# Raw attention pairs as four TensorE blocks, and TensorE in written order from the start: a sparse-attention and feed-forward kernel on one Trainium2 core

## The chip, the cores and the metric

The kernel runs on one core of a Trainium2 chip. The core has a matrix engine (TensorE, PE in the rows), a vector engine (VectorE, DVE), a scalar engine (ScalarE, ACT), a general engine (GpSimd, POOL) and a queue that starts transfers (SyncE, SP). Each engine works through its own list of instructions in the order in which they stand there, and waits on semaphores for the others. Matrix products go to PSUM, which has eight banks of 512 fp32 columns by 128 partitions; all other operands lie in SBUF. TensorE's clock is granted at one of two levels, 1.2 or 2.4 GHz.

The metric is the device time of one execution in microseconds (us), lower is better. The kernel before takes 1020.98 us, the median of three runs (1018.97 to 1024.09).

## The reference

Eight batches with eight heads each, head size 64. Each head has 512 local and 32 global tokens. A local token sees the 32 global ones and the local ones at a distance of up to 32; a global token sees all. The result of all heads is one row of 512 numbers per token, which goes through a feed-forward network with 2048 hidden units and a slope `alpha` for negative values.

```python
k_all = concatenate([k_g, k_l]); v_all = concatenate([v_g, v_l])
out_g = softmax(q_g @ k_all.T / 8) @ v_all
s_ll = where(abs(pos_q - pos_k) <= 32, q_l @ k_l.T / 8, -1e9)
out_l = softmax(concatenate([q_l @ k_g.T / 8, s_ll])) @ v_all
x = heads side by side, 4352 rows of 512
h = x @ w_in                              # 512 x 2048
g = maximum(h, 0) + alpha * minimum(h, 0)
return g @ w_out                          # 2048 x 512
```

## The kernel before

**The feed-forward part** is most of the work. The tokens form nine groups: the 512 local tokens of each batch, and at the end all 256 global ones. A group has 16 steps, one per 128 hidden units. Step `t` issues `f1(t)` (12 matmuls of 128 rows by 512 columns into a bank `h`: x and `w_in` are each split into a high and a low part, and three of the four products are added), then VectorE, ScalarE and GpSimd make `gh` and `gl` of it, and two steps later `f2(t)` (12 matmuls) adds into the four banks `o0` to `o3`. There are two `h` banks, two `s` banks for all of attention, and four `o` banks: eight in all.

**Weights.** There are 32 pieces of weights (f, j), each loaded as 64-bit words, decoded by two ScalarE, three VectorE and one GpSimd instruction (`decode_words`, L113 to L120), and split by one ScalarE and one GpSimd instruction (`split_weights`, L126, L127). `weights_step` decodes 11 pieces before step 0 and the other 21 in the first 14 steps.

**Attention** is done in pairs `P` of heads, 32 pairs, four to a batch. The main loop runs over units `u`; unit `u` holds step `t = u - 19`, so 19 units (the prelude) go ahead of step 0. Pair `P` begins in unit `4P`. The pairs 0 to 7 are "raw": they work in plain fp32 and transpose the probabilities on TensorE; the pairs from 8 on use another route, which the change leaves as it is. The pairs 0 to 3 are finished in the prelude, 4 to 7 in the first 17 steps.

A raw pair does the following. (1) Scores: for each of two heads and four chunks of 128 queries, two matmuls of 64 x 64 by 160 columns (`s_ps`), then a VectorE instruction that scales, masks and finds the minimum (L243), a ScalarE exponential (L247), a sum, a reciprocal (L209) and a ScalarE scaling (L214) into `p_sb`. Before, one unit does two chunks of one head in one bank, so a pair takes four score blocks in four units. (2) Eight TensorE transposes of `p_sb` (`pt`, L313), copied to `pt_sb` by ScalarE (L302), and VectorE transposes of the rest (L318). (3) The scores of the global tokens (`g_ps`) and their softmax in `sg_sb` (L270 to L280), two TensorE transposes of it (L286) and two copies. (4) The products with v (`pv_raw`, 24 matmuls into `o_ps`, in two halves in two units), and copies to `x_raw` and `x_glb`. `p_sb`, `pt_sb` and `sg_sb` exist once: pair P+1 can write each only when pair P has been read.

**What sets the order.** The program is traced unit by unit: `attn_pre`, `f1`, `attn_mid`, `f2` part 0, `attn_post`, `f2` part 1, `weights_step`. A scheduler with a timeline of its own then fixes each engine's list; what is inside `boost(u)` is preferred. From unit 36 on (`pinned`, `PIN`), the matmuls of the helper at L92 keep the order in which they are written; before that, and for the transposes, the scheduler may move them. In the prelude `keep_warm` issues four matmuls of zeros by 512 columns in each of 18 units, into the `h` banks.

```python
EV = dict(pt0=(2, "mid"), pt1=(4, "pre"), ptg=(4, "pre"), pv0=(5, "mid"), pv1=(6, "mid"))
BT = dict(s="s", g="o3", o="s", w="h")
```

These two lines give the unit of each raw event relative to `4P`, and the bank of each kind (in the prelude the transposes take `o0` to `o2`; from pair 4 on all take `s`).

## Time and profile before

| | |
|---|---|
| median of the runs | 1020.98 us |
| profiled execution | 1023.57 us |
| span of its trace | 1021.8 us |
| mean granted clock of TensorE | 0.979 of 2.4 GHz |
| TensorE busy with matmuls | 990.6 us, 97% |
| VectorE, ScalarE, GpSimd busy | 61%, 52%, 40% |

The span runs from the first to the last instruction of the trace; the execution's own time is 1.8 us longer. A matmul's busy time overlaps that of its neighbours, so steps are best read from start to start: in the steady part eight matmuls of 512 columns start 1.87 us apart in all, 0.234 us each. In a row of the timeline the first number is the start, the second the time to the end of the last instruction of the row, then engine, line and operation, `out<-in`, for a matmul rows x columns of the loaded block, the shape, and the count. An fp32 matmul of a raw pair appears as two passes, so a score block of four matmuls is a row with x8. A bracket gives the idle time ahead of the row and what ended it.

### The profile page before, as it was taken

The page shows a single profiled execution, that of the slowest core. Times are in us where ns is not written, and L with a number is a line of the kernel's source. Part 1 is how long each engine was busy: PE and PEld are TensorE (multiplying, and loading weights), DVE is VectorE, ACT ScalarE, POOL GpSimd, SP SyncE. Part 2 cuts the span into 40 slices and gives each one's busy share as a digit, 9 for nine tenths or more (in the row PEclk, how much of TensorE's full clock was granted, in tenths as well). Part 3 has the DMA queues.
Part 4 walks back from the last instruction along what each step waited for, and adds up shares of the span by engine and source line. Part 5 has one row for each costly group of instructions (what it writes and reads, how often), then busy time and mean ns, then how long its engine had stood idle before and what let it go on. Part 6 is the DMA issues. An engine that isn't in the chain of part 4 may idle for free.

```text
span 1021.8 us, 16979 instructions
## 1 busy us (share of the span) xinstructions
PE 990.6 (97%) x5592; PEld 793.0 (78%) x5592; DVE 625.8 (61%) x1999; ACT 532.9 (52%) x1491; POOL 413.5 (40%) x333
## 2 busy tenths in 40 slices
PE   7998998988999999999999999999999999999998
PEld 4565766766888888888888888888888888888798
DVE  7946868766666766676666666766667665322322
ACT  6767665675555655555556555555556543201121
POOL 6712666664344343334344344334434422222222
PEclk9897999989999999999999999999999999999999
DMA  9725233226454554555445544555455532100010
GB/s 348 263 65 209 94 113 115 70 65 192 140 152 140 169 152 146 149 155 175 140 146 158 181 143 143 151 160 156 130 152 177 154 109 86 42 1 1 1 42 22
DMA packets 95273, 133.00 MB, mean 130 GB/s; under 512 B 10192, under 2 KB 53712, under 8 KB 95184
## 3 DMA queue, kind: packets, MB, share of 16 engines
q1 hardware_dynamic: 95184, 131.91, 41.5%
q8 instruction: 44, 0.72, 0.3%
q14 instruction: 45, 0.37, 0.1%
HBM read 100.93 MB, written 30.93 MB: 129 GB/s over the span
## 4 chain that ended last, share of the span: by engine, by line
PE 85%; DVE 8%; ACT 4%; issue 2%; POOL 1%; DMA 0%; SPq 0%; DVEq 0%; POOLq 0%; ACTq 0%
PE o L93 35%; PE h_ps L93 35%; PE o_ps L93 6%; PE s_ps L93 5%; PE g_ps L93 3%; DVE wt L115 1%; DVE wt L118 1%; ACT p_sb L247 1%; PE warm L93 1%; DVE pt_sb L318 1%; DVE wt L117 1%; ACT wt L113 1%; DVE g L405 1%; DVE p_sb L243 0%; DVE g L406 0%
## 5 line engine op out<-in xcount | busy, mean ns | idle before, releaser
L93 PE MATMUL h_ps<-xh,wt 128*128 128x512 f32 (+1 forms) x1152 | 352.3, 388 | 1.4 <-DVE g L406 1.4
L409 POOL TENSOR_TENSOR gl<-g,gh 128x512 fp32r<-128x512 f32 (+1 forms) x144 | 178.4, 1239 | 422.7 <-ACT gh L408 377.2
L93 PE MATMUL o<-gh,wt 128*128 128x512 f32 (+1 forms) x1152 | 284.5, 389 | 5.1 <-ACT ost L302 3.6
L93 PEld LDWEIGHTS o<-gh,wt 128*128 128x128 f32 x1152 | 207.7, 190 | 52.5 <-ACT ost L302 4.6
L93 PEld LDWEIGHTS h_ps<-xh,wt 128*128 128x128 f32 x1152 | 207.3, 191 | 41.9 <-DVE g L406 1.7
L93 PE MATMUL h_ps<-xl,wt 128*128 128x512 f32 (+1 forms) x576 | 222.4, 387 | 1.0 <-DVE xl L388 0.9
L408 ACT CAST gh<-g 128x512 fp32r<-128x512 f32 (+1 forms) x144 | 85.4, 593 | 251.9 <-DVE g L406 243.7
L405 DVE TENSOR_SCALAR g<-h_ps,alpha_sb 128x512 f32<-128x512 f32 (+1 forms) x144 | 103.2, 717 | 142.3 <-PE h_ps L93 139.2
L93 PE MATMUL o<-gl,wt 128*128 128x512 f32 (+1 forms) x576 | 151.6, 384 | 0.0
L247 ACT ACTIVATE p_sb<-p_sb,mn 128x224 f32<-128x224 f32 (+2 forms) x256 | 115.1, 451 | 53.6 <-DVE mn L243 53.5
L214 ACT ACTIVATE p_sb<-p_sb,rz 128x192 f32<-128x192 f32 (+1 forms) x252 | 101.5, 452 | 70.6 <-DVE rz L209 64.9
L93 PEld LDWEIGHTS h_ps<-xl,wt 128*128 128x128 f32 x576 | 109.1, 190 | 26.1 <-DVE xl L388 1.8
L93 PEld LDWEIGHTS o<-gl,wt 128*128 128x128 f32 x576 | 104.9, 188 | 24.0 <-issue 0.6
L297 DVE STREAM_TRANSPOSE pt_sb<-sg_sb 32x64 f32<-32x64 f32 x384 | 90.5, 236 | 26.8 <-ACT sg_sb L280 21.5
L193 POOL TENSOR_TENSOR hi<-rawq,hi 64x512 fp32r<-64x512 f32 x48 | 62.4, 1300 | 90.5 <-DMA vt<-in_vt_dram 53.3
L406 DVE SCALAR_TENSOR_TENSOR g<-h_ps,g 128x512 f32<-128x512 f32 (+1 forms) x144 | 94.0, 653 | 3.0
L243 DVE CUSTOM_DVE_ANT_0 p_sb<-s_ps,mask 128x192 f32<-128x192 f32 x192 | 65.2, 369 | 28.8 <-PE s_ps L93 25.3
L196 POOL TENSOR_TENSOR kl<-rawk,hi 128x640 fp32r<-128x640 f32 x48 | 75.4, 1571 | 3.7
L93 PE MATMUL o_ps<-pt_sb,vt 128*64 128x160 f32 (+4 forms) x832 | 69.5, 289 | 2.7 <-ACT pt_sb L302 1.1
L209 DVE RECIPROCAL rz<-rz 128x2 f32<-128x2 f32 x128 | 20.8, 164 | 76.7 <-ACT rz L208 75.6
L93 PEld LDWEIGHTS o_ps<-pt_sb,vt 128*64 128x64 f32 (+2 forms) x832 | 49.4, 135 | 22.2 <-issue 14.8
L120 POOL TENSOR_TENSOR wt<-wt,wr 128x512 int32<-128x512 int32 x32 | 42.8, 1339 | 45.5 <-DVE wt L118 31.0
(85 smaller groups left out, 1055.0 us busy)
## 6 DMA issues: line engine op xcount, KB each, us to landing
scratch<-p_sb SPq DMA_DIRECT2D x192, 112.0 KB, 2.4
wraw<-in_w_dram SPq DMA_DIRECT2D x32, 512.0 KB, 7.1
vt<-in_vt_dram SPq DMA_DIRECT2D x32, 512.0 KB, 4.7
rawk<-in_qk_dram SPq DMA_DIRECT2D x96, 160.0 KB, 3.0
rawq<-in_qk_dram SPq DMA_DIRECT2D x96, 128.0 KB, 2.7
pt_sb<-scratch SPq DMA_DIRECT2D x48, 256.0 KB, 2.7
gn<-in_gn_dram SPq DMA_DIRECT2D x32, 304.0 KB, 4.9
pt_sb<-scratch SPq DMA_DIRECT2D x48, 192.0 KB, 2.9
```

What stands on the lines that cost most here:

```text
L93: ins = nc.tensor.matmul(*a, **k)
L120: nc.gpsimd.tensor_tensor(ti, ti, r, op=ALU.add)
L193: nc.gpsimd.tensor_tensor(q, raw[64:128], q.bitcast(F32), op=ALU.subtract)
L196: nc.gpsimd.tensor_tensor(kl[P, h], raw, t.bitcast(F32), op=ALU.subtract)
L214: nc.scalar.activation(r, r, AF.Copy, scale=rz[:parts, e : e + 1])
L243: nc.vector.tensor_tensor_reduce(out=pr, in0=s[:, 256 * e : 256 * e + nn], in1=masks[e], scale=-0.125, scalar=3.0e38, op0=ALU.add, op1=ALU ...
L247: nc.scalar.activation(pr, pr, AF.Exp, bias=mn[:, e : e + 1], scale=-1.0, accum_out=z[:, e : e + 1])
L297: nc.vector.transpose(dst, src)
L405: nc.vector.tensor_scalar(g[:, 0:n], h[:, 0:n], 0.0, alpha_sb[:, f : f + 1], op0=ALU.min, op1=ALU.mult)
L406: nc.vector.scalar_tensor_tensor(g[:, 0:n], h[:, 0:n], 0.0, g[:, 0:n], op0=ALU.max, op1=ALU.add)
L408: nc.scalar.copy(gh[:, 0:n], g[:, 0:n])
L409: nc.gpsimd.tensor_tensor(gl[:, 0:n], g[:, 0:n], gh[:, 0:n].bitcast(F32), op=ALU.subtract)
```

## The change

A raw pair becomes four blocks, one per unit, each with two whole banks, all in `attn_mid`. Unit `4P`: the scores of chunks 0, 1 and 2 of both heads, head 0 in one bank and head 1 in the other. Unit `4P+1`: chunk 3 of both heads, and in the second bank the two transposes of the previous pair's `sg_sb`. Unit `4P+2`: all products with v of the previous pair and this pair's global scores (the banks that the later pairs already use in that way). Unit `4P+3`: all eight transposes, one bank per head. In the prelude the blocks take `o0,o1`, `s,s`, `o2,o3`, `s,s` in turn; later all take the two `s` banks. All matmuls and transposes of the whole program keep their written order. The zeros become five matmuls in each of 19 units (95 in place of 72), behind the unit's block. A pair's softmax gets one sum and one reciprocal for six chunks and one for two; GpSimd scales three chunks of pair 0 in place of four.

```diff
-NWARM = 18
-WARM = (2, 2)
+NWARM = 19
+WARM = 5
-PIN = 36
     def matmul(*a, **k):
-        ins = nc.tensor.matmul(*a, **k)
-        if pinned[0]:
-            tc.keep_in_program_order(ins)
-        return ins
+        tc.keep_in_program_order(nc.tensor.matmul(*a, **k))
+
+    def transpose(*a):
+        tc.keep_in_program_order(nc.tensor.transpose(*a))
...
+    def pair_banks(u, names):
+        tags = {0: ("o0", "o1"), 2: ("o2", "o3")}.get(u % 4, "ss") if u < NPRE else "ss"
+        return [bank(tag, name) for tag, name in zip(tags, names)]
...
+    def scores_raw(P, chunks, banks):
+        for y, i in enumerate(chunks):
+            for h in range(2):
+                t = hi[P][64 * h : 64 * h + 64]
+                for f in range(2):
+                    q0, k0 = 128 * i + 64 * f, NQ + 160 * i + 64 * f
+                    matmul(banks[h][64 * f : 64 * f + 64, 160 * y : 160 * y + 160], t[:, q0 : q0 + 64], t[:, k0 : k0 + 160], start=True, stop=True)
...
+    def values_and_globals(P):
+        first, last = held.pop(P)
+        if live(P - 1):
+            (pv_raw if P - 1 < NRAW else pv_all)(P - 1, first, last)
+        if live(P):
+            global_scores(P)
+        if live(P - 1):
+            pv_out(P - 1, first, last)
...
+    def raw_block(u):
+        P, s = divmod(u, 4)
+        raw, glb = live(P) and P < NRAW, 0 <= P - 1 < NRAW
+        if s == 0 and raw:
+            banks = pair_banks(u, ("s_ps", "s_ps"))
+            scores_raw(P, (0, 1, 2), banks)
+            softmax_raw(P, (0, 1, 2), banks)
+        if s == 1 and (raw or glb):
+            banks = pair_banks(u, ("s_ps", "s_ps"))
+            if raw:
+                scores_raw(P, (3,), banks)
+            if glb:
+                transpose_glb(banks[1])
+            if raw:
+                softmax_raw(P, (3,), banks)
+            if glb:
+                copy_glb(banks[1])
+                global_transposes(P - 1)
+        if s == 3 and raw:
+            banks = pair_banks(u, ("pt", "pt"))
+            for h in range(2):
+                transpose_pe(h, banks[h])
+            for h in range(2):
+                copy_pe(h, banks[h])
...
     def attn_mid(u):
         P, s = divmod(u, 4)
-        glob(P, s, "mid")
-        while tails:
-            tails.pop()()
-        raw_events(u, "mid")
+        if s == 2 and (live(P) or live(P - 1)):
+            values_and_globals(P)
+        raw_block(u)
...
-        if u < NWARM:
-            keep_warm(WARM[0])
...
         if u < NWARM:
-            keep_warm(WARM[1])
+            keep_warm(WARM)
```

The first place is TensorE's list in the prelude, about pair 2 (`pt` are the transposes of `p_sb`, `s_ps<-ident` those of `sg_sb`). Before:

```order
L93 MATMUL s_ps<-qk_raw 64x160 x4
L93 MATMUL warm<-idle 128x512 x2
L93 MATMUL o_ps<-pt_sb,vt 64x96
L93 MATMUL warm<-idle 128x512 x2
L93 MATMUL s_ps<-qk_raw 64x160 x4
L93 MATMUL warm<-idle 128x512 x2
L313 MATMUL pt_509<-ident,p_sb 128x128 x2
L93 MATMUL warm<-idle 128x512 x10
L93 MATMUL g_ps<-gn 64x256 x2
L93 MATMUL g_ps<-gn 64x32
L93 MATMUL warm<-idle 128x512 x2
L313 MATMUL pt_509<-ident,p_sb 128x128 x2
```

The same place now:

```order
L84 MATMUL warm<-idle 128x512 x5
L87 MATMUL pt<-ident,p_sb 128x128 x8
L84 MATMUL warm<-idle 128x512 x5
L84 MATMUL s_ps<-qk_raw 64x160 x12
L84 MATMUL warm<-idle 128x512 x5
L84 MATMUL s_ps<-qk_raw 64x160 x4
L87 MATMUL s_ps<-ident,sg_sb 128x128 x2
L84 MATMUL warm<-idle 128x512 x5
L84 MATMUL o_ps<-pt_sb,vt 64x96 x2
L84 MATMUL o_ps<-pt_sb,vx 64x64 x2
L84 MATMUL o_ps<-pt_sb,vt 64x2x64 x2
L84 MATMUL o_ps<-pt_sb,vt 64x96 x2
```

The score blocks, which stood singly between warm-ups, are now one of twelve matmuls and one of four, the eight transposes stand together, every block has five warm-ups behind it, and the products with v follow the two transposes of `sg_sb`.

The second place is VectorE's list in the prelude at the end of the eleven weight pieces (`wt`, `wraw`; the last is the last of the L118 or L112 rows). Before:

```order
L357 TENSOR_REDUCE xgt<-o_ps 128x32
L270 TENSOR_REDUCE gm<-g_ps 128x1
L243 ISA p_sb,mn<-s_ps,rmask 128x160
L243 ISA mn 128x1
L243 ISA p_sb,mn<-s_ps,rmask 128x160
L243 ISA mn 128x1
L118 SCALAR_TENSOR_TENSOR wt<-wraw,wt 128x512
L358 TENSOR_TENSOR x_glb<-x_glb,xgt 128x32
L209 RECIPROCAL rz<-rz 128x2
L271 TENSOR_SCALAR gm<-gm 128x1
L243 ISA p_sb,mn<-s_ps,rmask 128x160
L243 ISA mn 128x1
```

Now:

```order
L109 TENSOR_SCALAR wt<-wt 128x512
L111 TENSOR_SCALAR wt<-wt 128x512
L112 SCALAR_TENSOR_TENSOR wt<-wraw,wt 128x512
L211 RECIPROCAL rz<-rz 128x6
L211 RECIPROCAL rz<-rz 128x2
L315 STREAM_TRANSPOSE pt_sb<-p_sb 32x4x32 x6
L366 TENSOR_REDUCE x_glb<-o_ps 128x32
L367 TENSOR_TENSOR x_glb<-x_glb,g_ps 128x32
L267 TENSOR_REDUCE gm<-g_ps 128x1
L268 TENSOR_SCALAR gm<-gm 128x1
L269 COPY gm<-gm 64x1
L270 TENSOR_TENSOR gm<-gm 64x1
```

Behind the last weight piece there stood scores of pair 2 (the ISA rows of `mn`) and the rest of pair 1's global softmax; now there stand the reciprocals and transposes of pair 1 first, and its whole global softmax behind the outputs of pair 0.

The third place is TensorE's list among the feed-forward steps (`h_ps` is f1, `o0` to `o3` are f2). Before, at scores of pair 6 and transposes of pair 5:

```order
L93 MATMUL h_ps_1602<-xl_1028,wt_1311 128x512
L93 MATMUL h_ps_1602<-xh_1031,wt_1311 128x512 x2
L93 MATMUL s_ps_1500<-qk_raw_1209 64x160 x4
L313 MATMUL pt1_1511<-ident_114,p_sb_71 128x128 x2
L93 MATMUL h_ps_1602<-xl_1032,wt_1311 128x512
L93 MATMUL h_ps_1602<-xh_1035,wt_1311 128x512 x2
L93 MATMUL h_ps_1602<-xl_1036,wt_1311 128x512
L93 MATMUL h_ps_1602<-xh_1079,wt_1311 128x512 x2
L93 MATMUL h_ps_1602<-xl_1080,wt_1311 128x512
L93 MATMUL o0_1285<-gh_1463,wt_1013 128x512
L313 MATMUL pt1_1511<-ident_114,p_sb_71 128x128 x2
L93 MATMUL o0_1285<-gh_1463,wt_1013 128x512
```

Now, at the second block of pair 5, between f1 and f2 of one unit:

```order
L84 MATMUL h_ps_1229<-xh_1057,wt_664 128x512 x2
L84 MATMUL h_ps_1229<-xl_1058,wt_664 128x512
L84 MATMUL s_ps_1249<-qk_raw_938 64x160 x2
L84 MATMUL s_ps_1250<-qk_raw_938 64x160 x2
L87 MATMUL s_ps_1250<-ident_114,sg_sb_73 128x128 x2
L84 MATMUL o0_1268<-gh_1110,wt_381 128x512 x2
L84 MATMUL o1_1269<-gh_1110,wt_381 128x512 x2
L84 MATMUL o2_1270<-gh_1110,wt_381 128x512 x2
L84 MATMUL o3_1271<-gh_1110,wt_381 128x512 x2
L84 MATMUL o0_1268<-gl_1111,wt_381 128x512
L84 MATMUL o1_1269<-gl_1111,wt_381 128x512
L84 MATMUL o2_1270<-gl_1111,wt_381 128x512
```

Attention stood at several places inside `f1` and `f2`; now one block stands between them, and the chunk's four matmuls alternate between two banks. From the first score block of pair 9 on, TensorE's list is the same in both programs.

## Rows read from the trace of the kernel before

**Rows 1.** Of the page: the busy time of each engine.

```profile
PE 990.6 (97%) x5592; PEld 793.0 (78%) x5592; DVE 625.8 (61%) x1999; ACT 532.9 (52%) x1491; POOL 413.5 (40%) x333
```

**Rows 2.** The view of stretches (start:end, length, busy time and instructions of PE, PEld, DVE, ACT and POOL, granted clock as a share of 2.4 GHz, DMA share, GB/s): the decoding of the first weights, the pairs 1 to 3 of the prelude from one end of the products with v to the next, the steps 2 to 15, and the steady part.

```profile
20.00:40.00 20.00, 18.20 (x112) 11.43 (x111) 19.26 (x48) 17.15 (x49) 14.29 (x13) 1.00 0.77 291
...
34.40:62.90 28.50, 26.95 (x153) 16.66 (x152) 18.55 (x61) 18.99 (x61) 14.72 (x11) 0.82 0.48 173
62.90:74.90 12.00, 11.86 (x106) 7.83 (x104) 6.91 (x35) 10.43 (x39) 1.29 (x1) 1.00 0.32 98
74.90:86.60 11.70, 10.05 (x101) 6.32 (x99) 6.94 (x38) 9.32 (x35) 1.27 (x1) 1.00 0.46 149
96.40:226.00 129.60, 119.84 (x691) 89.92 (x689) 96.22 (x232) 84.17 (x214) 87.23 (x66) 0.93 0.27 91
262.00:900.00 638.00, 638.00 (x3513) 523.87 (x3512) 404.04 (x1373) 340.65 (x958) 244.40 (x180) 1.00 0.48 143
```

**Rows 3.** TensorE's timeline: the start of f1(2), the price of f1 and f2 (eight matmuls of `f2`, and the next matmul), and the first score block of pair 9.

```profile
96.43 1.22 PE L93 MATMUL h_ps<-xh,wt 128*128 128x512 f32 x2
...
197.03 2.03 PE L93 MATMUL o<-gh,wt 128*128 128x512 f32 x8
198.90 0.40 PE L93 MATMUL h_ps<-xh,wt 128*128 128x512 f32 x1
...
230.39 0.33 PE L93 MATMUL s_ps<-hi 128*128 128x192 f32 x1 [0.48 <-DVE mn L243]
```

**Rows 4.** TensorE's waits from 96 to 246 us by what ended them (total us, times, longest). One more, at 243 us, is left out.

```profile
PE s_ps L93 <- DVE mn L243: 2.5, 2, 2.0
PE pt L313 <- DVE mn L243: 2.4, 1, 2.4
PE s_ps L93 <- ACT pt_sb L302: 1.7, 1, 1.7
PE o L93 <- ACT gh L408: 1.5, 2, 1.3
PE h_ps L93 <- DVE g L406: 1.4, 1, 1.4
PE o_ps L93 <- DVE mn L243: 0.8, 1, 0.8
```

**Rows 5.** The view of stretches again, about the changes of the clock (columns as in rows 2): pair 1, the start of the steps, and a short stretch behind one of the waits of rows 4.

```profile
43.00:55.00 12.00, 11.98 (x46) 6.94 (x46) 7.39 (x28) 7.67 (x28) 10.02 (x8) 0.57 0.54 206
...
89.00:101.00 12.00, 11.48 (x41) 7.67 (x38) 9.06 (x29) 8.17 (x27) 4.68 (x4) 0.50 0.74 283
...
212.00:217.00 5.00, 5.00 (x15) 3.93 (x15) 1.07 (x4) 3.58 (x12) 4.88 (x5) 0.50 0.10 32
```

**Rows 6.** VectorE's timeline: the last instruction of the eleventh weight piece.

```profile
43.74 0.77 DVE L118 SCALAR_TENSOR_TENSOR wt<-wraw,wt 128x512 uint32<-128x512 uint32 x1
```

**Rows 7.** TensorE's timeline in the prelude: warm-ups at full clock, warm-ups at half clock (x10), the six passes of global scores, and the products with v of pair 1 from the first to the last.

```profile
34.63 4.06 PE L93 MATMUL warm<-idle 128*128 128x512 f32 x14
38.54 0.38 PE L286 MATMUL pt<-ident,sg_sb 128*128 128x128 f32 x2
...
51.77 3.67 PE L93 MATMUL warm<-idle 128*128 128x512 f32 x10
55.38 0.73 PE L93 MATMUL g_ps<-gn 128*64 128x256 f32 x6
56.04 0.73 PE L93 MATMUL warm<-idle 128*128 128x512 f32 x2
...
59.68 0.30 PE L93 MATMUL o_ps<-pt_sb,vt 128*64 128x96 f32 x1
...
62.90 0.73 PE L93 MATMUL warm<-idle 128*128 128x512 f32 x2
```

**Rows 8.** TensorE's timeline: a score block alone, and four transposes, among the steps.

```profile
128.95 0.76 PE L93 MATMUL s_ps<-qk_raw 64*64 64x160 f32 x8
129.64 0.44 PE L313 MATMUL pt<-ident,p_sb 128*128 128x128 f32 x2
...
161.07 0.60 PE L313 MATMUL pt<-ident,p_sb 128*128 128x128 f32 x4
161.43 0.48 PE L93 MATMUL h_ps<-xh,wt 128*128 128x512 f32 x1
```

**Rows 9.** TensorE's timeline where a score block of head 1 (operands in the partitions 64 to 127) and the last products with v (partitions 0 to 63) follow one another.

```profile
187.78 0.35 PE L93 MATMUL s_ps<-qk_raw 64*64 64x160 f32 x2
187.93 0.28 PE L93 MATMUL o_ps<-pt_sb,vt 64*64 64x128 f32 x2
187.97 0.57 PE L93 MATMUL s_ps<-qk_raw 64*64 64x160 f32 x6
188.47 0.50 PE L93 MATMUL o<-gl,wt 128*128 128x512 f32 x1
```

**Rows 10.** ScalarE's timeline: two exponentials of 160 columns, one behind the other, and four scalings.

```profile
78.63 0.41 ACT L247 ACTIVATE p_sb<-p_sb,mn 128x160 f32<-128x160 f32 x1
...
79.04 0.41 ACT L247 ACTIVATE p_sb<-p_sb,mn 128x160 f32<-128x160 f32 x1
...
81.79 1.38 ACT L214 ACTIVATE p_sb<-p_sb,rz 128x160 f32<-128x160 f32 x4
```

**Rows 11.** VectorE's waits from 96.4 to 230.4 us, the longest group (columns as in rows 4).

```profile
DVE wt L115 <- ACT wt L113: 14.3, 12, 2.4
```

More of the change, by code (lines that the diff above doesn't have):

```diff
@@ L247, in local_scores, with tail, softmax_raw, global_bank @@
             nc.scalar.activation(pr, pr, AF.Exp, bias=mn[:, e : e + 1], scale=-1.0, accum_out=z[:, e : e + 1])
-        return lambda: softmax_tail(ranges, z, 2, pool)
+        def tail():
+            nc.scalar.activation(rz[:, 0:n], z[:, 0:n], AF.Copy, bias=1e-9)
+            nc.vector.reciprocal(rz[:, 0:n], rz[:, 0:n])
+            for e, (_, _, r) in enumerate(parts):
+                if e < npool:
+                    nc.gpsimd.tensor_scalar(r, r, rz[:, e : e + 1], 1.0, op0=ALU.mult, op1=ALU.mult)
+                else:
+                    nc.scalar.activation(r, r, AF.Copy, scale=rz[:, e : e + 1])
+        tails.append(tail)
+    def local_scores(P, h, a):
+        s = bank("s", "s_ps")
+        parts = []
+        for e in range(2):
+            i = 2 * a + e
+            n, c0 = 32 * WBLK[i], 32 if i == 0 else 0
+            q, k0 = hi[P, h][:, 128 * i : 128 * i + 128], WSTART[i]
+            o = s[:, 256 * e : 256 * e + n]
+            matmul(o, q, hi[P, h][:, NQ + k0 : NQ + k0 + n], start=True, stop=False)
+            matmul(o, q, kl[P, h][:, k0 : k0 + n], start=False, stop=True)
+            parts.append((o, mask[:, c0 : c0 + n], sub_ap(p_sb, 0, 128, 896 * h + 4 * c0 + 32 * i, ((128, n // 32), (1, 32)))))
+        softmax(parts)
+    def scores_raw(P, chunks, banks):
[5 more added lines that the diff above has]
+                    matmul(banks[h][64 * f : 64 * f + 64, 160 * y : 160 * y + 160], t[:, q0 : q0 + 64], t[:, k0 : k0 + 160], start=True, stop=True)
+    def softmax_raw(P, chunks, banks):
+        parts = []
+        for h in range(2):
+            for y, i in enumerate(chunks):
+                c = 896 * h + 160 * i
+                parts.append((banks[h][:, 160 * y : 160 * y + 160], rmask[:, (0, 1, 1, 2)[i], :], p_sb[:, c : c + 160]))
+        softmax(parts, 3 if P == 0 and len(chunks) == 3 else 0)
     gbank = {}
-    def global_bank(P):
-        bank = s_bank(P, "g")
-        s = bank[:, 0:288] if P < NRAW else bank[:, 160:448]
+    def global_bank(P, bk):
+        s = bk[:, 160:448]
         if live(P):
@@ L333, in fetch_pt, with pv_raw @@
             nc.sync.dma_start(sub_ap(pt_sb, 0, n, 1280 * t + 640 * h, ((1, 512),)), sc[128 * t : 128 * t + n])
-    def pv_raw(P, a):
-        b, p = divmod(P, NPAIR)
+    def pv_raw(P, first, last):
         v = vts[P]
-        ob = s_bank(P, "o")
-        o = ob.rearrange("p (e n) -> p e n", e=2)
-        for e in range(2):
-            i = 2 * a + e
+        for i in range(4):
+            ob, o0 = (first, 160 * i) if i < 3 else (last, 0)
             tail = ((1, 160),) if i == 3 else ((96, 2), (1, 64))
@@ L495, in attn_mid @@
         P, s = divmod(u, 4)
-        glob(P, s, "mid")
-        while tails:
-            tails.pop()()
-        raw_events(u, "mid")
+        if s == 2 and (live(P) or live(P - 1)):
+            values_and_globals(P)
+        raw_block(u)
+        if P >= NRAW:
+            while tails:
+                tails.pop()()
         if s == 0 and live(P):
@@ L518, in attn_post @@
         P, s = divmod(u, 4)
-        glob(P, s, "post")
-        raw_events(u, "post")
+        if live(P) and s == 2:
+            global_softmax(P)
+        while tails:
+            tails.pop()()
         if s % 2 == 1 and live(P) and P >= NRAW:
```

150 lines of the change are left out of this document (36 added, 114 removed).

## The prediction

> **What bounds the kernel now.** I read the busy times first: TensorE has matmuls in flight 97% of the span, the other engines 40 to 61% [rows 1]. Then the stretches, to see where TensorE is not full. From 262 to 900 us it is busy 638 of 638 us at full clock, so nothing is to be had there; what is open lies before, in the prelude and in the steps 2 to 15 (119.8 of 129.6 us, mean clock 0.93) [rows 2]. Then the order of instructions: from the first score block of pair 9 on, TensorE's list is the same in both programs, and by then both have done f1(0) to f1(16) and f2(0) to f2(14). That block starts at 230.39 us [rows 3]. So the change is worth what it moves this one point, which I call the milestone; behind it I assume the same pace. Last the timeline and the waits ahead of it, in two parts, cut where f1(2) starts at 96.43 us [rows 3].
>
> In the prelude the first 40 us belong to VectorE, which decodes weights: 19.3 of 20 us busy from 20 to 40 [rows 2]. Its eleventh weight piece ends at 44.5 [rows 6]. Behind it a pair takes 12.0 and 11.7 us [rows 2], a chain that passes TensorE, VectorE and ScalarE in turn. In the steps TensorE waits 10.3 us in all up to the milestone, 7.4 of it for the one `p_sb` or for banks that a minimum or a copy has yet to read (2.5 + 2.4 + 1.7 + 0.8) [rows 4]. Cold clock adds to that: 0.93 means that 0.14 of 129.6 us went at half speed, 18.1 us, of which half, 9.1 us, is lost. 4.6 us of the cold time are the start, up to 101 us, the rest follows waits, as at 212 [rows 2, 5]; so 2.3 us of loss are inherited and 6.7 are made by the steps.
>
> **The prelude, part by part.** The transposes of pair 1 now stand in TensorE's list behind everything of pair 0 and ahead of all scores of pair 2; on VectorE the reciprocals that they need come behind the eleventh weight piece. Eight scalings of 0.32 follow [rows 10]. In the new order VectorE has fewer rows ahead of that piece, so its end lies between about 40 and 44.5; with 2.6 us behind it pt(1) can start at 44 to 48, and I take 46. From there the written order makes a cycle per pair, at full clock:
> - eight transposes of 0.09 (four in 0.36) [rows 8]: 0.72;
> - five warm-ups of 0.28 (14 in 3.91) [rows 7]: 1.40;
> - the block of twelve score matmuls, 24 passes of 0.086 (eight in 0.69) [rows 8]: 2.07 if they run singly, half of it, 1.04, if the two heads run side by side;
> - then ScalarE: eight exponentials of 0.41 [rows 10], and, estimated as two and a bit more instructions of that length, 0.5 from the last score to the first of them and 0.4 for the copies of `sg`'s transposes, which are queued behind them and without which the products can't start: 4.2. Ten warm-ups, chunk 3 and two transposes lie beside it on TensorE (1.4 + 0.35 + 0.2 + 1.4 = 3.4), so they cost nothing at full clock;
> - the products with v: 3.22 [rows 7];
> - global scores 0.66 [rows 7] and five more warm-ups 1.40.
>
> The sum is 12.6, against 12.0 and 11.7 before. At half clock each term of TensorE doubles, and the ten warm-ups no longer hide behind ScalarE (6.8 against 4.2): 1.4 + 2.8 + 2.1 + 6.8 + 6.4 + 1.3 + 2.8 = 23.6.
>
> The two heads do run side by side, by the row where eight passes of head 1's scores and four of the products lie together: 0.69 us from 187.78 to 188.47, as much as a score block alone [rows 8, 9]. They use the two halves of the rows. The two halves of the columns give nothing: a score block alternates between them and still pays 0.086 a pass. The Trainium skill has it otherwise (TensorEngine Tiling (Array Packing), "Theoretical Speedup"): in its table, with 64 x 64 tiles both dimensions count. By that rule twelve matmuls would take a quarter of the single time, an estimate of 0.52 us; no row shows more than two at once, so the sum goes by 1.04.
>
> Before, the clock fell at the same place: 0.57 from 43 to 55 [rows 5], and ten warm-ups took 0.36 each there rather than 0.28 [rows 7]. The new list has nothing that may run ahead while pt(1) waits for VectorE, so TensorE stands idle before 46. I take the first cycle at half clock up to the middle of the products, and full clock from there on, as from 62.9 before [rows 2]: 46 + 1.4 + 2.8 + 2.1 + 6.8 = 59.1, + 4.8 = 63.9 for the end of PV(1) (62.9 before); + 12.6 twice = 89.1 for PV(3) (86.6 before); + 0.66 + 1.4 puts f1(0) at 91.2. Before, f1(0) and f1(1) were threaded into the prelude's gaps; now 24 matmuls of 0.234 [rows 3], the transposes of pair 4 and a block of twelve scores stand in line: 7.6 us, f1(2) at 98.8. Against 96.43 that is **+2.4**. Bounds: full clock throughout and pt(1) at 44 gives f1(2) at 89.5, **-6.9**; half clock throughout from 48 gives about 126, **+30**.
>
> **From f1(2) to the milestone**, 134.0 us before. 360 matmuls of f1 and f2 cost 84.2 and stay. Attention before: ten score blocks of 0.69, 32 transposes of 0.09, four pairs of products and globals at 3.88, pair 8's scores about 1.8, together 27.1. After: nine shares of four matmuls, side by side, at 0.345 = 3.1; 32 transposes 2.9; the products and pair 8 as before; 23.3, so -3.8. Left of the 134.0, with idle 10.3 and clock 9.1 taken off, are 3.3 us, for 21 places where the list goes from feed-forward to attention and back; there are 12 now, which at 0.16 each gives -1.4. Work: **-5.2** (if the heads do not run side by side, 3.1 less).
>
> Idle and clock: the 7.4 us of waits and the 6.7 us of cold clock behind them, 14.1, are what the one-block-per-unit order could remove, since each block has a unit of feed-forward work, 5.6 us, between it and the one that needs its result. It could also remove nothing: the copies and exponentials still queue on ScalarE behind the `gh` and weight work, and with fixed order a late one holds all that follows. I take half, **-7**, with 0 and -14 as ends.
>
> Sum: +2.4 - 5.2 - 7 = -9.8; the profiled execution of 1023.57 becomes 1013.8. The median of the runs lies 2.6 below that execution, so the forecast is **1011 us**.
>
> **The rivals.**
> - *All of it works.* Full clock in the prelude and no wait left: -6.9 - 5.2 - 14.1 = -26.2, 995. For it speaks that among the steps 24 matmuls of other work stand between two blocks; against it that pair 1's stretch was cold before too. Half way lies 1003.
> - *One more cold cycle.* The clock comes back with PV(2) rather than PV(1): 23.6 - 12.6 = +11.0, 1022.
> - *VectorE becomes the bound of the steps.* It was busy 96.2 of 129.6 us there [rows 2] and waited 14.3 for ScalarE's half of the decoding [rows 11]: 110.5 of 129.6 are spoken for, and its work doesn't shrink. If TensorE's gain turns into waiting for `g` and minima, the steps stay at 134.0, and only the prelude's +2.4 is left: 1023. The Trainium skill says as much (TensorEngine Tiling (Array Packing), "PSUM Bottleneck"): tiles speed up the products, not the reading of PSUM. The rows bear it out as far as VectorE's share goes; TensorE's waits named a minimum for 5.7 of 10.3 us.
> - *Slower: warm-ups pinned into a chain at half clock.* They now stand between a pair's blocks whatever waits, 95 x 0.28 = 26.6 us of matmul time at full clock and twice that at half; if the chip does not grant the full clock before the steps, the cycles of pairs 2 and 3 cost 23.6 too and the ten hidden warm-ups lie bare: +22 on the forecast, 1033. It decides as soon as a pair's 4.2 us on ScalarE are shorter than what TensorE needs beside them. For it: the clock stood at 0.57 in pair 1 with warm-ups all about [rows 5]. Against: it came back and was 1.00 from 62.9 to 86.6 [rows 2].
>
> **How the numbers follow.** Forecast 0.40, with 1004 to 1018 as its own range (3 us if the heads do not overlap, 7 either way on the waits); all of it 0.15; one more cold cycle 0.12; VectorE 0.18; all cold 0.15. About 0.5% is what a measurement of this kernel can tell from no change, so faster is below 1015.9 and slower above 1026.1. Faster: 0.15 and nearly all of the forecast, 0.52. Same: the forecast's upper edge, most of VectorE's case and of one cold cycle, 0.28. Slower: all cold and the tails of these two, 0.20. The range of 8 in 10 leaves out the last of the best case and half of the all-cold one: 997 to 1032.
>
> **What would show it.** In the changed kernel's timeline: pt(1) at 44 to 48; cycles of 12.6 us (right) or near 23.6 (the slower rival), with the granted clock of 45 to 92 beside them; f1(0) at about 91; twelve score matmuls in about 1.04 us, not 2.07 or 0.52; among the waits of the steps those of `s_ps` and `pt` for `mn` and `pt_sb` shorter or gone, and VectorE's busy share there near 0.75 or near 0.9; the milestone near 221. It is wrong at the root if the steady part behind the milestone changes its pace.

## The result, and the profile after

The changed kernel takes 1025.45 us (median of 20 runs, 1022.50 to 1030.68); the kernel before, in 20 runs, 1018.72 (1013.44 to 1024.09). The ratio is 1.0070, 95% interval 1.0052 to 1.0088: slower by some 7 us, where 1011 us was forecast. The profiled execution took 1027.97 us (span 1026.2), against 1023.57 (1021.8) before.

The two spans differ by 4.4 us, and that splits at three places. First TensorE's timeline of the changed kernel, with f1(2), the milestone (the score block of pair 9), the same list's block 27 us later, and two blocks far apart in the steady part:

```profile
104.10 0.50 PE L84 MATMUL h_ps<-xh,wt 128*128 128x512 f32 x1
...
236.66 0.25 PE L84 MATMUL s_ps<-hi 128*128 128x192 f32 x1
...
263.78 0.25 PE L84 MATMUL s_ps<-hi 128*128 128x192 f32 x1
...
351.18 0.27 PE L84 MATMUL s_ps<-hi 128*128 128x224 f32 x1
...
703.65 0.27 PE L84 MATMUL s_ps<-hi 128*128 128x224 f32 x1
```

The same instructions in the kernel before (f1(2) and the milestone stand in [rows 3]), with a wait that lies between them:

```profile
243.53 2.86 PE L93 MATMUL o<-gh,wt 128*128 128x512 f32 x8 [3.64 <-ACT ost L302]
...
263.01 0.25 PE L93 MATMUL s_ps<-hi 128*128 128x192 f32 x1
...
350.01 0.27 PE L93 MATMUL s_ps<-hi 128*128 128x224 f32 x1
...
700.93 0.27 PE L93 MATMUL s_ps<-hi 128*128 128x224 f32 x1
```

| | before | after | later by |
|---|---|---|---|
| f1(2) | 96.43 | 104.10 | 7.7 |
| milestone | 230.39 | 236.66 | 6.3 |
| 27 us on | 263.01 | 263.78 | 0.8 |
| span | 1021.8 | 1026.2 | 4.4 |

So the prelude lost 7.7 us. The steps won 1.4 up to the milestone, and 5.5 more just behind it: there the kernel before waits 3.64 us for the outputs' copies and the clock falls behind the wait, and the changed one does neither. And then, with one list of instructions in both and full clock in both, the changed kernel loses another 3.6 us, evenly: from the 350 us row to the 700 us row the same instructions take 350.91 us before and 352.47 after (from the starts in nanoseconds; the rows are rounded).

The stretches of the changed kernel (columns as in [rows 2]):

```profile
20.00:40.00 20.00, 9.23 (x55) 5.95 (x56) 17.47 (x45) 14.46 (x40) 12.80 (x10) 0.67 0.99 389
34.40:62.90 28.50, 21.54 (x168) 14.14 (x169) 17.92 (x56) 19.69 (x67) 13.75 (x11) 0.68 0.33 122
...
75.00:90.00 15.00, 13.88 (x136) 9.10 (x134) 6.71 (x38) 11.18 (x41) 1.27 (x1) 1.00 0.36 117
90.00:100.00 10.00, 10.00 (x55) 7.09 (x54) 5.44 (x18) 4.13 (x12) 1.29 (x1) 0.66 0.56 189
```

From 20 to 40 us TensorE has 9.2 us of work where it had 18.2 [rows 2]: nothing may pass the waiting products of pair 0. The clock stands at 0.67 there and falls to half again at 60 and at 90. The prelude in TensorE's timeline: the products of pair 0, pair 1's transposes, then one full cycle, from the transposes of pair 3 to f1(0):

```profile
39.88 0.59 PE L84 MATMUL o_ps<-pt_sb,vt 128*64 128x96 f32 x3 [10.77 <-ACT pt_sb L286]
...
49.06 1.28 PE L87 MATMUL pt<-ident,p_sb 128*128 128x128 f32 x8
...
79.94 1.03 PE L87 MATMUL pt<-ident,p_sb 128*128 128x128 f32 x8
80.73 1.59 PE L84 MATMUL warm<-idle 128*128 128x512 f32 x5
82.25 1.05 PE L84 MATMUL s_ps<-qk_raw 64*64 64x160 f32 x24
83.22 1.62 PE L84 MATMUL warm<-idle 128*128 128x512 f32 x5
...
88.11 0.55 PE L84 MATMUL o_ps<-pt_sb,vt 128*64 128x96 f32 x3 [1.12 <-ACT pt_sb L286]
...
92.38 1.27 PE L84 MATMUL g_ps<-gn 128*64 128x256 f32 x6
93.58 2.50 PE L84 MATMUL warm<-idle 128*128 128x512 f32 x5
95.88 1.06 PE L84 MATMUL h_ps<-xh,wt 128*128 128x512 f32 x2
```

TensorE's waits from 96 to 246 us after the change (columns as in [rows 4]):

```profile
PE pt L87 <- ACT sg_sb L272: 8.4, 3, 5.1
PE h_ps L84 <- ACT wt L120: 3.1, 1, 3.1
PE h_ps L84 <- POOL wt L121: 2.4, 1, 2.4
PE o_ps L84 <- ACT pt_sb L286: 1.1, 1, 1.1
```

The waits for minima (`mn`) of [rows 4] are gone, as intended. In their place the transposes wait for an exponential of the global softmax. The longest of these, on three engines:

```profile
182.10 0.73 PE L84 MATMUL g_ps<-gn 128*64 128x256 f32 x6
...
188.50 0.60 PE L87 MATMUL pt<-ident,p_sb 128*128 128x128 f32 x4
194.15 1.12 PE L87 MATMUL pt<-ident,p_sb 128*128 128x128 f32 x4 [5.05 <-ACT sg_sb L272]
```

```profile
189.65 0.45 DVE L267 TENSOR_REDUCE gm<-g_ps 128x1 f32<-128x288 f32 x1
```

```profile
193.52 0.48 ACT L272 ACTIVATE sg_sb<-g_ps,gm 128x288 f32<-128x288 f32 x1
```

Four transposes go at once, into the bank of the products. The other four need the bank of the global scores (`g_ps`), which were ready at 182.8. VectorE takes their maximum only at 189.65, behind weights and its own transposes, and ScalarE the exponential at 193.52, behind a rounding of keys and three weight instructions.

### The profile page after: what moved, and what is told of

It is laid out like the page before. It is cut to its first block, busy times and chain, and to the rows that moved or that the text cites. A ratio compares the mean times of both kernels' runs of the same rounds, so it can differ in the third digit from the quotient of the medians.

```text
span 1026.2 us, 16973 instructions
## 1 busy us (share of the span) xinstructions
PE 980.9 (96%) x5615; PEld 792.2 (77%) x5615; DVE 624.0 (61%) x1975; ACT 528.3 (51%) x1476; POOL 410.9 (40%) x332
## 4 chain that ended last, share of the span: by engine, by line
PE 83%; DVE 7%; ACT 5%; issue 2%; DMA 1%; POOL 1%; SPq 0%; DVEq 0%; ACTq 0%; POOLq 0%
PE h_ps L84 35%; PE o L84 34%; PE o_ps L84 5%; PE s_ps L84 4%; PE g_ps L84 3%; ACT p_sb L207 2%; DVE wt L112 1%; DVE wt L109 1%; DVE wt L111 1%; PE warm L84 1%; ACT p_sb L216 1%; DMA wraw<-in_w_dram 1%; ACT wt L107 1%; DVE g L395 1%; DVE pt_sb L315 1%
## 5 line engine op out<-in xcount | busy, mean ns | idle before, releaser
L84 PE MATMUL o_ps<-pt_sb,vt 128*64 128x160 f32 (+3 forms) x768 | 62.1, 294 | 15.6 <-ACT pt_sb L286 15.6
L84 PEld LDWEIGHTS o_ps<-pt_sb,vt 128*64 128x64 f32 (+2 forms) x768 | 45.8, 138 | 32.5 <-ACT pt_sb L286 17.2
L211 DVE RECIPROCAL rz<-rz 128x2 f32<-128x2 f32 (+1 forms) x112 | 18.5, 165 | 74.6 <-ACT rz L210 73.7
```

The lines of the kernel that those rows point to most:

```text
L84: tc.keep_in_program_order(nc.tensor.matmul(*a, **k))
```

## Experiments

Four questions: what slows the steady part; what makes the prelude late; what the transposes' wait costs; what two heads side by side are worth. Ratios below are against the kernel before in the same set, which stood at medians of 1017.06, 1017.73, 1018.88 and 1019.22 us.

**1. The pace, on one chip.** The kernel before and the changed one, unedited:

> The kernel before, unchanged, against itself, for the spread and for the pace of TensorE in the steady part on this chip. Behind 280 us successive matmuls of f1 or f2 start 0.2333 us apart in the trace of before and 0.2347 in that of after, at full clock in both. If the program makes the pace (theory P, by where its weights lie), it is 0.2333 here again. If it is the chip or the day (theory Q), this run and the run of the changed kernel beside it have one pace. Ratio 1.000 by either.

> The changed kernel, unchanged, for a trace on the same chip. Theory P: 0.2347 us a matmul in the steady part. Theory Q: the same pace as the kernel before in this set. The steps' waits should be those seen at first: transposes for the bank of the global scores 5 to 9 us, weights 3 to 6 us.

Against itself the kernel before came to 1.0001 (0.9967 to 1.0035). The same instructions as above, some 350 us apart, took 350.91 us in it and 352.47 in the changed kernel, as in the first traces to a hundredth. The pace belongs to the program. The changed kernel's one run took 1025.68 us. In this second trace of it f1(2) came at 101.14 us, since the clock did not fall at 90. Six traces in all, with four of later runs, have the changed kernel's list of TensorE in the prelude: f1(2) lies between 98.39 and 106.80 in them, and between 90.39 and 96.45 in three traces with the list of before. So the prelude is later throughout, but by how much differs with the clock of the execution.

**2. Where the weights lie.** Without `xgt`, three buffers of 128 bytes a partition, all weight buffers of the changed kernel begin 384 bytes lower: the first at byte 92960 of a partition, before at 93344. Both are 32 bytes past a multiple of 64; past a multiple of 256 they are 32 and 160. The edit puts the three buffers back:

```diff
+        if P == 0:
+            for _ in range(3):
+                nc.vector.memset(small("xgt", 32)[:, 0:1], 0.0)
```

> The changed kernel with the three small xgt buffers of the kernel before allocated again (three tiny memsets beside it), so that the weights and the raw keys lie at the addresses of before, 384 bytes higher. Theory P, that the addresses make the steady pace: 0.2333 us a matmul again, and about 4 us less than the changed kernel, ratio about 1.003. Theory Q: no change, ratio 1.007.

1021.95 us, ratio 1.0028 (1.0001 to 1.0055) in place of 1.0070, and the pace is that of before, 350.91 us:

```profile
353.34 0.27 PE L84 MATMUL s_ps<-hi 128*128 128x224 f32 x1
...
704.26 0.27 PE L84 MATMUL s_ps<-hi 128*128 128x224 f32 x1
```

The other way round, the kernel before with `xgt` moved above the weights, so that these fall by 384 bytes:

```diff
+    late = ctx.enter_context(tc.tile_pool(name="late", bufs=1))
...
-            tmp = small("xgt", 32)
+            tmp = late.tile([128, 32], F32, tag="xgt", name="xgt", bufs=3)
```

> The kernel before with its xgt buffers moved above the weights and nothing else, so that the weights and raw keys lie where the changed kernel has them, 384 bytes lower. Theory P: 0.2347 us a matmul in the steady part in place of 0.2333, about 4 us slower, ratio 1.004. Rival: it needs something else of the changed kernel too; then 0.2333 and ratio 1.000.

It takes on the slow pace, 352.47 us:

```profile
342.31 0.27 PE L94 MATMUL s_ps<-hi 128*128 128x224 f32 x1
...
694.78 0.27 PE L94 MATMUL s_ps<-hi 128*128 128x224 f32 x1
```

The interval of its ratio, 1.0016 (0.9992 to 1.0041), is too wide to show the 4 us by itself, but holds them. Its trace also shows what the prelude of before can do: the clock never fell there, and f1(2) came at 90.39 us, 6 us sooner than in the trace that the prediction used. Then three more places:

> The changed kernel with the three buffers and 96 bytes more below the weights, which then begin at a multiple of 64 bytes (of 128, not of 256) rather than at an odd multiple of 32. Theory P1, that a row's place within 64 bytes sets the pace: another pace than 0.2333 and 0.2347 us a matmul, below 0.2333 if aligned is better. Theory P2, that only where the weights lie against the other operands in larger steps matters: 0.2333 or 0.2347 again.

> As the run before this one, with the weights 64 bytes higher (an odd multiple of 32 still, another place within 256 bytes), to see a fourth pace: 0.2333, 0.2339 to 0.2345 and 0.2347 us were seen at 160, 0 and 32 bytes within 256. If only the place within 64 bytes counted, 32, it would be one of the two paces seen there, and these differ, so I expect a value of its own between 0.231 and 0.236.

> The changed kernel with its weights 128 bytes higher, at 160 bytes within 256 as in the kernel before, but not at its addresses. Theory P3, the place within 256 bytes sets the pace: 0.2333 us a matmul. Theory P4, the distance to something else or a larger period counts: another value.

| first weight at | past a multiple of 256 | the same instructions | runs of |
|---|---|---|---|
| 93344 | 160 | 350.91 | before; three buffers |
| 93088 | 160 | 350.91 | changed, 128 bytes higher |
| 93408 | 224 | 351.52 | 64 bytes above those of before |
| 93440 | 0 | 351.69 | changed, 480 bytes higher |
| 92960 | 32 | 352.47 | changed; before, moved down |

The run 480 bytes higher took 1020.98 us, ratio 1.0033 (1.0000 to 1.0066), the one run 128 bytes higher 1019.02; the spread of the times hides these steps, the traces show them. P3 holds where it was tried: 160 past a multiple of 256 gives one time at two addresses. P1 falls: the places 32 past a multiple of 64 have three different times, and the aligned one (93440 is a multiple of 256 too, other than its expectation says) is not the best. The run 64 bytes higher is the first kernel of experiment 6 with its weights moved; at 1015.47 us, ratio 0.9960 (0.9935 to 0.9985), it stands 1.8 us above that one, where 0.61 us per 351 over the last 760 us would make 1.3.

Raw queries and keys and the low parts of the keys (`kl`) shift along with the weights, but the traces tell them apart: f1 and f2 read none of these, and the buffers of x, `gh` and `gl` begin at the same places in all runs. Within the 351 us the 572 steps from one f1 matmul to the next add up to 133.58 us in the kernel before and 134.50 in the changed one, the 572 from one f2 matmul to the next to 134.77 and 135.26, and the 637 inside attention to 49.67 and 49.56. So at least 1.4 of the 1.56 us arise where the weights are the only operand that moved. Why 160 is the best of the five places is open.

**3. The prelude: is it the fixed order?** Matmuls and transposes keep their order only from step 0 on:

```diff
+        pinned[0] = u >= NPRE
```

> The changed kernel with the written order kept only from step 0 on; in the prelude the scheduler may move the same blocks and the same 95 warm-ups. Theory A, that the loss of the prelude (f1(2) at 104.1 against 96.4 us) is the fixed order's, since TensorE stands idle behind the waits of the pairs 0 and 1 and the clock falls four times: f1(2) back near 96, and the time 5 to 8 us below the changed kernel, ratio 1.000. Rival: the blocks themselves make the chain of a pair longer (one late softmax for six chunks); then f1(2) stays above 101 and the ratio above 1.004.

1035.45 us, ratio 1.0147 (1.0103 to 1.0192). Theory A falls: left free, the scheduler puts up to thirteen warm-ups in a row and single transposes between others, and f1(2) comes at 110.59 us. The written order is the better of the two for these blocks; since the list is another one, the run does not show that the blocks make a pair's chain longer.

**4. Is it the cold clock?** More warm-ups where TensorE stood idle (the weights are at the addresses of before in this run and all later ones, but for those on addresses):

```diff
-            keep_warm(WARM)
+            keep_warm({2: 18, 5: 40}.get(u, WARM))
```

> The changed kernel with the weights at the addresses of before, and more warm-ups where TensorE stood idle in the prelude: 18 in place of 5 in unit 2, 40 in place of 5 in unit 5, ahead of the products of pair 0. Theory A2, that the prelude is late by the cold clock that follows these waits: full clock from about 16 to 50 us, pt(1) at 47 to 48 in place of 49.1, f1(2) some 4 us sooner, ratio about 0.999. Rival A3, that the chain of a pair through ScalarE and VectorE sets the prelude: the clock is full and f1(2) moves by less than 1.5 us, ratio 1.003.

1022.35 us, ratio 1.0049 (1.0027 to 1.0072): no gain. In its trace pt(1) is at 43.5 us, 5.6 sooner, yet f1(2) at 100.02, 1.1 sooner than in the second trace of the changed kernel. The clock was full up to 56 us. Then it stood at half for some 10 us, behind waits for the chain of pair 1 (its parts of the two groups below are 1.8 and 2.6 us), and pair 1's cycle took 20.7 us, from 43.46 to 64.14:

```profile
PE o_ps L84 <- ACT pt_sb L286: 4.6, 3, 2.6
PE s_ps L87 <- ACT sg_sb L277: 3.5, 2, 1.8
```

```profile
57.00:66.00 9.00, 9.00 (x54) 6.29 (x51) 3.26 (x13) 3.16 (x8) 1.28 (x1) 0.50 0.30 95
```

The cycle of pair 3, at full clock:

```profile
78.72 1.03 PE L87 MATMUL pt<-ident,p_sb 128*128 128x128 f32 x8
...
92.49 0.62 PE L84 MATMUL h_ps<-xh,wt 128*128 128x512 f32 x2
```

```profile
78.70:92.50 13.80, 12.68 (x118) 8.33 (x117) 6.73 (x39) 10.39 (x37) 0.93 (x1) 1.00 0.39 123
```

13.8 us at clock 1.00. So A3 has the better of it: the chain of a pair took back what the earlier start had won. But the clock, full before 56 us, was not full behind it, and this run does not show a prelude without cold clock. The run 128 bytes higher of experiment 2 comes nearest: no warm-up was added there, the clock was full from 50 us on, and f1(2) came at 98.39, sooner than with the waits filled.

**5. Which part of the chain?** First the warm-ups, moved to where TensorE waits:

```diff
+            keep_warm({2: 18, 5: 40}.get(u, (5, 9, 0, 0)[u % 4]))
```

> As the run before (18 and 40 warm-ups), and in the other units of the prelude the warm-ups stand where TensorE waits for copies anyway: 9 behind chunk 3, 5 behind the chunks 0 to 2, none behind the products and the transposes. Theory A4, that the five warm-ups behind the products and behind the transposes lie in the chain of a pair, 1.4 us each at full clock: a pair's cycle gets 2.8 us shorter, f1(2) 6 to 8 us sooner than in the run before if the clock holds, ratio about 0.992. Rival: without them the clock falls in each cycle and the cycle is no shorter.

1018.83 us, ratio 1.0005 (0.9980 to 1.0031), f1(2) at 96.86: 3.5 us less by median than in run 4. But not by the way expected, since a cycle is no shorter: the transposes of pair 2 and pair 3 start at 60.02 and 74.69 us, 14.7 apart. The rival has its part: the clock fell again in the cycles of the pairs 2 and 3, at 68 and 82 us. What is new are 13.1 us of waits, here up to 96 us:

```profile
PE s_ps L87 <- ACT sg_sb L277: 13.1, 4, 4.7
```

The transposes of `sg_sb` wait for the global softmax, a chain that the warm-ups had mostly covered. The second wait of the changed kernel, that of the transposes for the bank of the global scores, is for the same chain, so the last edit shortens it: the exponential is taken of the score itself, which leaves out five VectorE instructions that find the maximum. The softmax is the same but for rounding. In the form for all eight raw pairs:

```diff
+        if P < NRAW:
+            nc.scalar.activation(sg_sb, s[:, 0:288], AF.Exp, scale=0.125, accum_out=z[:, 0:1])
+        else:
...
```

First for the pairs 4 to 7 alone (`NRAW // 2 <= P < NRAW`), with the warm-ups as they were, as a test of the steps (a run of the same set as the last two):

> The changed kernel with the weights at the addresses of before (as in the run with the three buffers), and for the pairs 4 to 7 the global softmax without its maximum: five VectorE instructions between the global scores and ScalarE's exponential are left out, so that the bank of the global scores comes free sooner (the exponential is of the score itself; the softmax is the same but for rounding). Theory B, that TensorE's new waits in the steps are the second four transposes waiting for this bank, which VectorE's queue holds: their 8.5 us between 104 and 236 us fall below 2, and the time by 6 to 9 us with the clock that follows, ratio about 0.995. Rival: VectorE and ScalarE are the bound there anyway and the wait moves to the weights (h_ps for wt, now 5.5 us); then waits stay at 13 to 15 us and the ratio at 1.003.

1015.69 us, ratio 0.9984 (0.9953 to 1.0015): 6.3 us less than with the maximum by the medians (1021.95), 4.5 by the two ratios, whose intervals touch. With the moved warm-ups the times scatter less, and the same cut takes 1018.83 to 1013.69 (experiment 6), with the intervals apart. The wait for the bank is gone from the list, and the whole list from 96 to 246 us is down from 15.0 us to 9.3:

```profile
PE h_ps L84 <- POOL wt L121: 3.3, 2, 2.5
PE o_ps L84 <- ACT pt_sb L289: 2.7, 2, 2.0
PE s_ps L84 <- DVE mn L203: 1.6, 2, 0.9
PE h_ps L84 <- ACT wt L120: 1.3, 1, 1.3
PE h_ps L84 <- DVE g L402: 0.4, 1, 0.4
```

Theory B holds, though the ratio misses the 0.995 that it named. The rival is right in a small way: waits for weights stay at 4.6 us.

**6. Together.** The cut for the pairs 4 to 7 with the moved warm-ups, then the cut for all eight raw pairs:

> The two edits that helped, together: weights at the addresses of before, global softmax of the pairs 4 to 7 without its maximum, and the warm-ups of the prelude taken out of the chain of a pair (18 and 40 in the two early waits, 9 and 5 behind the score blocks, none behind products and transposes). If the bank wait in the steps and the warm-ups in the prelude are separate losses, their gains against the run with the three buffers add: 6.3 + 3.1 us, 1012 to 1013, ratio about 0.995. If the steps are bound by VectorE and the weights, an earlier start in the prelude is given back there: 1016, ratio 0.998.

> As the first of this set, and the global softmax of the pairs 0 to 3 is without its maximum as well. If the prelude's pairs now wait for this chain (TensorE waited 13.1 us for the scaled sg_sb in the run with the moved warm-ups), a pair gets about 1 us shorter and f1(2) comes 2 to 4 us sooner. If ScalarE's eight exponentials set the cycle, nothing moves.

1013.69 us, ratio 0.9942 (0.9918 to 0.9966), and 1009.94 us, ratio 0.9901 (0.9865 to 0.9937). The two gains add but for 1.1 us (8.3 of 6.3 + 3.1), and the cut in the prelude is worth 3.8 more. In the last trace the waits for the scaled `sg_sb` ahead of 96 us are down to 5.3 us, and f1(2) is at 93.35, 3.0 sooner than in the trace ahead of it. The cycle of pair 2 is 11.1 us, at full clock, but the two beside it, with cold clock in both, are 20.4 and 14.5:

```profile
60.12 1.09 PE L87 MATMUL pt<-ident,p_sb 128*128 128x128 f32 x8
...
71.23 0.98 PE L87 MATMUL pt<-ident,p_sb 128*128 128x128 f32 x7
```

This version beats both kernels. One more run asks whether the kernel before would win as much by the same cut:

> The kernel before, with the global softmax of the raw pairs 0 to 7 without its maximum, the edit that gave the block form 3.8 + 6.3 us. If that chain is long in both kernels, the kernel before gains 3 us or more as well (ratio 0.997 or less). If the chain binds only because the blocks put one bank of the global scores and one block of transposes a unit apart, it gains under 2 us, ratio 0.998 to 1.001.

1019.11 us, ratio 0.9991 (0.9954 to 1.0027): no gain by median. The interval leaves room for up to 4.7 us, so a small one is not excluded; the 10 us that the two cuts gave the block form (6.3 and 3.8) are. Why there is none is not shown. In its trace the steps, from f1(2) to the milestone, did get 10.1 us shorter (123.9 us, 134.0 before):

```profile
102.99 0.79 PE L93 MATMUL h_ps<-xh,wt 128*128 128x512 f32 x1
...
226.90 0.25 PE L93 MATMUL s_ps<-hi 128*128 128x192 f32 x1
```

But f1(2) came 6.6 us later than before, and the stretch of 32.6 us behind the milestone took 36.7. With the edit the free scheduler laid out another list (671 of TensorE's first 914 matmuls stand elsewhere), so the run does not tell the cut from the new order.

**7. Heads side by side.** The loop over heads put outside the loop over chunks, weights at the addresses of before:

```diff
-        for y, i in enumerate(chunks):
-            for h in range(2):
+        for h in range(2):
+            for y, i in enumerate(chunks):
```

> The changed kernel with the weights at the addresses of before and the score matmuls of a block ordered head by head, so that matmuls on the two halves of the rows no longer alternate. By the prediction's step (heads side by side take half the time) the block of 24 passes takes 2.07 us in place of 0.98, and the attention of the steps 3 us more. Rival: it is only a long block that runs fast; then 0.98 again.

The block, from its first pass to the warm-up behind it, takes 1.30 us:

```profile
66.76 1.37 PE L84 MATMUL s_ps<-qk_raw 64*64 64x160 f32 x24
68.06 0.50 PE L84 MATMUL warm<-idle 128*128 128x512 f32 x1
```

Neither answer. Heads in turn take 0.97 (82.25 to 83.22 above), heads apart 1.30, and 2.07 is nowhere. Its one run took 1015.3 us, less than each of the ten of its counterpart with three buffers (1019.11 to 1026.90); this was not followed up.

## Why the prediction was wrong

The terms of the sum, in us of the profiled executions:

| term | forecast | measured |
|---|---|---|
| prelude | +2.4 | +7.7 |
| work of the steps | -5.2 | -4.7 |
| idle and clock of the steps | -7 | +3.3 |
| behind the milestone | 0 | -1.9 |
| sum | -9.8 | +4.4 |

The step that failed most is idle and clock of the steps, then the prelude.

*That the pace behind the milestone stays the same* was an assumption of the first paragraph, and the one named as wrong at the root if it failed. It failed: 1.56 us per 351, 3.6 us from 263 us to the end, by the place of the buffers and not by any instruction. Putting the place back takes the ratio from 1.0070 to 1.0028. Nothing in the order of instructions or the timeline of before could show it; the allocation could, since the change drops `xgt`, but no row said that it matters. That the term still came out at -1.9 is luck: the wait at 243 us, which [rows 4] left out, went away with the change (5.5 us with its clock), and the sum had not counted on it. The three traces of before's list have it, with 3.6 to 4.9 us; why the changed kernel has none was not tried.

*The prelude* was put at +2.4 and measured +7.7 in the first trace, +4.7 in the second. The step "pt(1) can start at 44 to 48, and I take 46" gave 49.1. VectorE's end of it held: the eleventh piece was done at 44.7 and `p_sb` scaled by 47.2. But TensorE was not there yet: it stood 10.8 us ahead of the products of pair 0, which the step did not price, for copies that wait behind eight exponentials and weights on ScalarE, and then did these products at half clock. The cycle of 12.6 us measures 13.8 at full clock: from the end of twelve scores to the products it is 4.9 us and not 4.2, and the products take 3.5 (74.33 to 77.82 for pair 2) and not 3.22. "Full clock from there on" held in neither trace of the unedited changed kernel: in both it fell at 60 us, in the first at 90 again (0.66 from 90 to 100). Where it did hold, in the run 128 bytes higher, f1(2) came at 98.39, close to the 98.8 of the forecast, but by luck: pt(1) was 2.9 us late and two cycles 1.2 us long each, and a first cycle of 14.3 us, for the 20.0 that the step had at half clock, made up for them. Of the 7.7 us between the first traces the clock from 40 us on is the lesser part, by an estimate from the two rows below: it lost 0.18 of 64.1 us after and 0.17 of 56.4 before, 11.5 us against 9.6.

```profile
40.00:96.43 56.43, 51.78 (x366) 32.37 (x365) 34.22 (x152) 39.99 (x141) 15.48 (x12) 0.83 0.47 162
```

```profile
40.00:104.10 64.10, 60.41 (x464) 40.51 (x464) 33.55 (x148) 41.31 (x135) 16.73 (x14) 0.82 0.31 103
```

The claim that the ten warm-ups hide behind ScalarE is right and was drawn too small: they also hide most of the global softmax, which the step left out. Once the warm-ups were moved the cycle stayed at 14.7 us, or 14.0 at full clock (the first run of experiment 6), and TensorE waited for that softmax in it.

*The work of the steps*, -5.2, was close. From f1(2) to the milestone 132.6 us remain. Less 15.0 of idle time, and 8.0 of clock (0.06 of 132.56 us, by the mean clock of 0.94 in the row below), that is 109.6; before, 134.0 less 10.3 and 9.4 (0.07) is 114.3. So -4.7, to what the rounded clock allows.

```profile
104.10:236.66 132.56, 117.55 (x700) 89.77 (x697) 104.48 (x252) 86.67 (x228) 87.15 (x68) 0.94 0.34 110
```

*Idle and clock of the steps*, -7, is the step that failed: waits rose by 4.7 us (15.0 against 10.3), the loss to the clock fell by 1.4, and the +3.3 lies outside the ends that the step gave itself, 0 and -14. "Each block has a unit of feed-forward work, 5.6 us, between it and the one that needs its result" holds for the minima, which are gone, but the transposes' second bank is that of the global scores. Its way through VectorE's maximum and ScalarE's exponential took 11 us in the worst case, not 5.6. The warning that a late one holds all that follows stood in the text as the zero end; it should have been worked out for this bank. Cutting the chain returned 6.3 us by median, and took the waits to 9.3 us, about the 10.3 of before: it undid the new loss and did not bring the gain that the step claimed. Of the rivals, VectorE as the bound came nearest in kind: it was busy 104.5 of 132.6 us and its queue made the wait (the maximum at 189.65 above), but as the order of its queue, not as its share. The slower rival, a prelude all at half clock, did not come about: its cycle would have been 23.6 us, and 13.7 to 17.3 were seen in the six traces with this list.

*The base.* The forecast took 2.6 us off the profiled execution; by 20 runs it lies 4.9 above the median, because the clock fell in that execution's prelude as it does not in all: among the other executions of this kernel, 1015.16 us went with a mean clock of 0.992, 1025.01 with 0.980.

*What came out right*: two heads side by side halve the block, 0.97 against 1.04 forecast. But the price of undoing it is 0.33 a block, not 1.0, and "the two halves of the columns give nothing" is wrong. In the block at 82.25 us the passes start four at a time (82.250, 82.257, 82.264, 82.270), and the next four 0.186 and then 0.136 us behind. In a block of one head, [rows 8], they start two at a time (128.946, 128.953) at the same distances. That these two are the halves of the columns shows where one half is free: the last matmul of the global scores has no neighbour there, and its two passes start 0.027 us apart (78.299, 78.326); the four ahead of it, which have one, start in twos 0.007 us apart. So the 0.086 a pass already held two at once. The estimate of 0.52 is not reached, since it took a quarter of a price that was halved already. By the Trainium skill (TensorEngine Tiling (Array Packing), "Theoretical Speedup") small tiles count in both dimensions, and this trace agrees, with four passes at once.

## What to carry to other kernels

When a fixed order lets one bank pass from one user to the next, work out for each bank how long its slowest reader takes, with all that stands ahead of it in the readers' queues, and not only the reader that was late before. Before a cold clock or a fixed order is blamed, fill the waits and see whether the end moves: here the transposes of pair 1 came 5.6 us sooner and the end stayed, since the chain of the pair took it back. Before a price read from a row is halved, look at the single starts: some of the work in it may lie side by side already. And when two programs with one list of instructions run at two paces, compare the addresses of the matmuls' operands.

## What the runs showed of the hardware

The start of the weight buffers, moved by 64 to 480 bytes, changes TensorE's pace at full clock between 350.91 and 352.47 us for the same instructions, repeatable to 0.01 us. At least 1.4 of the 1.56 us between the ends lie in f1 and f2, whose only moved operand is the weights; which property of the address does it is open beyond the table above.

Matmuls of 64 x 64 blocks run four at once, on the two halves of the rows and of the columns, as read from their starts at full clock: 24 passes of 160 columns in six groups of four, 0.136 us apart but for 0.186 ahead of the second, and 12 passes on one half of the rows in six groups of two at the same distances.

With the heads apart, the passes of head 1 began 0.34 us after those of head 0 and ran beside them until 0.73, though head 0's twelve passes stand ahead in the list: its starts are 66.763, 66.949, 67.085, ... to 67.493 us, those of head 1 67.098, 67.284, 67.420, ... to 67.828. So TensorE did not start them in the order of its list: a later matmul on the free half of the rows passed waiting ones of the other half, and three groups of passes of head 0 (67.221, 67.357, 67.493) started behind it. That is why a block with the heads apart costs 1.30 us and not twice 0.97. What held head 1 back for the first 0.34 us is open.
